# A fused attention and FFN kernel: distances spread by TensorE, single bias loads, four copies on VectorE, rounds 0 and 1 in other orders

## Chip, cores and metric

One core of a Trainium2 chip. The metric is device time in microseconds, the median of several runs; lower is better. In the text PE is TensorE, DVE is VectorE, ACT is ScalarE, POOL is GpSimd and SP is SyncE, which here only issues DMAs.

## What is computed

Attention with a bias made by a small MLP from the logarithm of the distance, then a softplus feed-forward network over the result. Shapes: 4 batches, 8 heads, 576 positions, head size 64; the MLP has 32 hidden units; the network goes 512 to 2048 to 512.

```python
x = log1p(|i - j|) / log1p(max(i, 1))          # 576 x 576
bias = relu(x[..., None] @ w1 + b1) @ w2        # one 576 x 576 map for each of 8 heads
attn = softmax(q @ k.T / 8 + bias)
o = attn @ v                                    # to 2304 x 512
h = o @ w_in
out = (max(h, 0) + log1p(exp(-|h|))) @ w_out
```

## The kernel before

The program is one long straight line of instructions. The author writes the order of each engine by hand, so every engine works strictly in the order of the text, and an instruction that waits holds up all that stands behind it on its engine. SP's DMA issues are such a queue too.

**Start.** Three small DMAs bring the MLP's weights (`wts`, line 188), the row of 576 log distances copied to all 128 partitions (`dist`, line 189) and a table (`tab`, line 190). DVE makes `lw` (distances times w1, line 198), `pb1` (line 199) and `coef` (line 200) of them. All later work of the bias hangs on `lw`.

**Bias stage.** 36 steps, `s` from 0 to 35, make 16 rows of all 8 bias maps each. DVE or ACT makes four relu tiles `m` for a step (lines 220 and 222), PE multiplies them with `coef` into an accumulator `acc` in PSUM (line 235; two of these), ACT copies it in two pieces into a tile `e` (line 256; five of these), and SP stores `e` to a scratch `e_d` in HBM (line 260). The bias is read back from `e_d` in tiles of 128 rows: tiles 0 to 3 are the first head of a pair, 5 to 8 the second, tile 4 the last 64 rows of both (lines 305, 307, 309, 310). Each tile needs eight steps of the store to have landed. Tiles 0 and 5, 1 and 6, 2 and 7 are loaded in pairs after steps 10, 18 and 26. Tiles 3, 8 and 4 stand behind the loop in the text.

Into the late steps the first scores of attention are woven (`STAGE`). A number `wt` there means round `w`, tile `t`. `D` computes scores on PE (line 346), adds the bias and finds the row maximum on DVE (line 364) and takes the exponential on ACT (line 382). `R` computes the scores and only copies them out of PSUM, on ACT (line 357), to be finished later.

**Rounds.** Attention runs in rounds 0 to 16; round `n` is one batch of one pair of heads. A round is written as a string of tokens, each a few instructions. `S`, `A`, `X` and a digit are scores (PE), bias and maximum (DVE) and exponential (ACT) of one tile of the next round; `Z`, `ZA`, `ZX` the same for the round itself. `T` with two digits is a set of transposes on PE, `V` the copy of the result to SBUF, on ACT (`/a`, line 315) or DVE (`/d`, line 317). `P` is a product with v (line 469); `P3` and `P4` belong to the round before. `I` inverts the row sums on DVE (lines 507, 508), and needs the round's nine exponentials. `R` transposes them on PE, `C` copies them on ACT (line 523) and stores them to `r_d` in HBM (line 524). A third step reads them back, spread over 64 partitions each, by three DMAs into a tile `rb` (line 530): in rounds 0 and 1 on ACT's queue, later on SP's. `O` multiplies the accumulated product of the round before with its `rb` on DVE (line 489), which frees the accumulator `o` in PSUM for PE. Four DMAs then store the result to `x_d` (lines 495 to 498). `L` is a small copy on POOL, `B` one step of preparing FFN weights, `D6` and `D14` are 6 and 14 transposes of the identity with no use of their result, `k`, `q`, `v`, `w`, `b` are loads, `G` is the `rb` load, `Y` the store of the result, `W` a store of prepared weights.

Rounds 2 to 13 all use the same string `ROUND`; rounds 0 and 1 have their own, with their loads placed by position (`LOADS0`, `LOADS`). Where a round is not in `STEADY`, the reading back of `rb` is put off by 24 tokens from `C`, the store of the result by 8 tokens from `O`, and the store of prepared weights by 8 tokens from `B4`:

```python
STEADY = range(2, 17)
...
            if tok == "C" and n not in STEADY:
                defer(RB_AFTER, lambda n=n: units["r", n][2]())   # RB_AFTER = 24
```

**FFN.** From about 270 us on, PE multiplies without a break (lines 784 and 842).

Of the kernel before, what the change touches and what calls it, by code (L numbers as in the profile page):

```python
# [51 lines left out]
SETS = ((2, 4), (3, 8), (7, 5, 6), (1, 0))  # L52

ROUND0 = """
A6 A2 Z7 T10/1 A7 Z3 T20/0 V20/a T30/o A0 T00/2 ZA7 V00/d V30/a V10/a A1 A5 D6 Z8 X7 X2 ZX7 ZA3 X5
X6 ZA8 A3 ZX3 ZX8 Z4 ZA4 ZL1 ZL3 ZX4 A8 D14 T22/2 T40/1 T32/o ZL4 V32/d T02/0 V22/a V02/a T01/o X0
T11/2 V40/d T21/1 V11/a ZL2 V01/d V21/d L2 T12/0 P0 X8 L0 X1 I V12/d T41/1 A4 P1 X4 T31/0 R/2
V41/a C P2 V31/d L3 X3 L4 L1
"""

ROUND1 = """
I S4 T20/0 S3 A4 T11/1 A3 T00/2 S2 P3 X4 V00/d V20/a T02/0 V11/d T12/2 V02/a R/1 C P4 T41/0 S7
T22/1 S0 A2 O V12/a T01/o V41/a T10/0 V22/d L4 B0 T21/2 V01/a X3 A7 S1 V10/d P0 V21/a A0 T31/0
X2 T32/2 S5 X7 A1 P1 S6 V31/a V32/d X0 S8 B1 T30/1 X1 B2 L0 A5 T40/0 V30/a B3 L1 A8 V40/a X8 A6
X6 L3 P2 B4 X5 L2
"""

ROUND14 = """
# [56 lines left out]
def tile_log_bias_attention__then__softplus_ffn(  # L125
# [139 lines left out]
    N = 16  # L265
# [53 lines left out]
    def u_s(n, t):  # L319
# [187 lines left out]
        nc.vector.tensor_scalar(s_, s_, 1e-9, None, op0=ALU.add)  # L507
        nc.vector.reciprocal(s_, s_)

    def queue(n):  # L510
        return nc.scalar if n < 2 else nc.sync

    def u_r(n):

        st_ = {}

        def pe(on=None):
            assert ("i", n) in done
# [17 lines left out]
        return pe, first, second  # L536
# [33 lines left out]

    units = {}

    def raw_(w, t):
        unit = units["s", w, t] = u_s(w, t)
        return [((1,), unit[0], unit[3])]

    def emit(n, tok):

# [26 lines left out]
        elif kind in ("R", "C"):  # L605
            stage(("r", n), u_r, "RC".index(kind), *on)
        elif kind == "O":
            if n:
                stage(("x", n - 1), u_x, 0)
                if n not in STEADY:  # L610
                    defer(8, lambda: stage(("x", n - 1), u_x, 1))
        elif kind == "B":
            i = min(n, N - 1) - 1
            if 0 <= i < len(pre):
                stage(("b", i), u_bits, *a)
                if a[0] == 4 and n not in STEADY:
                    defer(8, lambda: stage(("b", n - 1), u_bits, 5))
        elif kind in ("k", "q"):
            emit_load(n + 3, kind)
        elif kind == "v":  # L620
            emit_load_v(n + 2)
        elif kind == "w":
            pre_load(n)
        elif kind == "b":
            if tiles:
                emit_bias(*tiles.pop(0))
        elif kind == "G":
            units["r", n][2]()
# [338 lines left out]
    for n in range(N + 1):  # L967
        tiles = [(n // B + 1 + (n % B == 3), t) for t in SETS[n % B]]
        if n < 3:
            tiles = [(1, t) for t in ((), range(5), range(5, 9))[n]]  # L970
        if n == 1:
            assert not s_held
            s_use[0] = 0
        toks = {0: ROUND0, 1: ROUND1, N - 2: ROUND14, N - 1: ROUND15, N: ROUND16}.get(n, ROUND).split()
        for i, tok in enumerate(toks):
            load = {0: LOADS0, 1: LOADS}.get(n, LOADS if n > N - 2 else {}).get(i)
            if load in ("k", "q"):
                emit_load(n + 3, load)
            elif load == "v":
                emit_load_v(n + 2)  # L980
            elif load == "v1":
                emit_load_v(n + 1)
            elif load == "w":
                pre_load(n)
            elif load == "b" and tiles:
                emit_bias(*tiles.pop(0))
# [88 lines left out]
```

## Time and profile before

| | us |
|---|---|
| median of 3 runs | 678.45 (677.08 to 681.55) |
| the profiled execution | 677.26 |
| its span, first to last instruction | 675.5 |
| granted TensorE clock over the span | 0.991 of 2.4 GHz |
| PE, ACT, DVE busy | 642.0, 512.2, 499.2 |

The span falls into four parts: the start (to 7 us), the bias stage (to 62 us), 17 rounds (to some 270 us) and the FFN. All times below are from the profiled execution, counted from its first instruction. Busy times of PE are modelled, so a PE that is shown busy need not be at its peak.

### The profile page before, as it was taken

The numbers are of one execution on the slowest core, as the hardware profiler recorded it, in microseconds if no ns is written. First come the engines' busy times: TensorE is split into PE (matmuls) and PEld (weight loads), VectorE is DVE, ScalarE is ACT, GpSimd is POOL, SyncE is SP. The second block draws the span as 40 slices with busy tenths as digits, with TensorE's granted clock in tenths as the row PEclk, the third lists the DMA queues.
The fourth block names the chain that finished last, engine by engine and source line by source line (L and its number), as shares of the span: only waits on it lengthen the run. The fifth ranks groups of instructions, "written<-read, shape, count | busy, mean of one in ns | idle before, by whom it ended". The sixth has DMA issues, their size and how long they took to land.

```text
span 675.5 us, 13207 instructions
## 1 busy us (share of the span) xinstructions
PE 642.0 (95%) x4807; PEld 478.2 (71%) x4807; DVE 499.2 (74%) x1082; ACT 512.2 (76%) x1058; POOL 38.0 (6%) x106
## 2 busy tenths in 40 slices
PE   5689779999999998899999999999999999999997
PEld 2124447667667665588888888888888888888886
DVE  6986668999999997779785965796774555556564
ACT  6898769999999997677776867786775665665654
POOL 0000111111111111100000000000000000000000
PEclk9989799999999999999999999999999999999999
DMA  4876948879788545451410305030300502204020
GB/s 146 298 266 221 360 137 277 264 251 297 248 266 278 179 149 187 154 187 64 155 64 32 125 1 188 31 125 14 112 1 0 187 1 93 95 0 156 0 95 32
DMA packets 51041, 96.85 MB, mean 143 GB/s; under 512 B 7440, under 2 KB 19104, under 8 KB 50976
## 3 DMA queue, kind: packets, MB, share of 16 engines
q1 hardware_dynamic: 50208, 95.34, 41.9%
q8 instruction: 38, 0.62, 0.4%
q10 hardware_dynamic: 768, 0.66, 0.3%
q14 instruction: 27, 0.22, 0.1%
HBM read 67.98 MB, written 28.01 MB: 142 GB/s over the span
## 4 chain that ended last, share of the span: by engine, by line
PE 89%; ACT 5%; DMA 3%; DVE 2%; issue 1%; ACTq 1%; SPq 0%; DVEq 0%
PE y L842 29%; PE h L784 29%; PE o L469 10%; PE s L346 6%; PE s L410 4%; PE acc L235 4%; PE t L346 3%; ACT p L382 2%; PE t L410 1%; ACT e L256 1%; DMA e_d<-e 1%; PE o L346 1%; PE o L410 1%; DMA dist<-in_c_dist_dram 1%; ACTq L530 0%
## 5 line engine op out<-in xcount | busy, mean ns | idle before, releaser
L784 PE MATMUL h<-x,wi 128*128 128x512 f32 (+1 forms) x960 | 212.5, 370 | 2.0 <-DVE wi L757 1.4
L842 PE MATMUL y<-wo,g 128*128 128x512 f32 x864 | 209.7, 391 | 0.0
L784 PEld LDWEIGHTS h<-x,wi 128*128 128x128 f32 x960 | 169.1, 189 | 36.4 <-DVE wi L757 2.6
L842 PEld LDWEIGHTS y<-wo,g 128*128 128x128 f32 x864 | 161.2, 188 | 33.7 <-DVE g L816 0.2
L807 DVE SCALAR_TENSOR_TENSOR u<-u,e 128x512 f32<-128x512 f32 (+1 forms) x80 | 50.9, 637 | 104.9 <-ACT l L804 104.7
L382 ACT ACTIVATE p<-p,m 128x576 f32<-128x576 f32 x144 | 110.4, 768 | 5.3 <-DVE m L364 1.8
L800 ACT ACTIVATE e<-h 128x512 f32<-128x512 f32 (+1 forms) x80 | 44.2, 553 | 80.4 <-PE h L784 80.4
L469 PE MATMUL o<-pt,vn 128*64 128x256 f32 (+3 forms) x640 | 82.9, 419 | 1.2 <-DVE pt L317 1.2
L364 DVE CUSTOM_DVE_ANT_0 p<-s,b 128x576 f32<-128x576 f32 x79 | 58.4, 753 | 9.7 <-ACT e L256 3.3
L814 ACT ACTIVATE g<-l 128x512 fp32r<-128x512 f32 (+1 forms) x80 | 46.8, 585 | 20.3 <-DVE l L811 10.7
L346 PE MATMUL s<-kn,qn 64*128 64x288 f32 (+1 forms) x416 | 58.5, 415 | 0.2 <-ACT p L357 0.2
L469 PEld LDWEIGHTS o<-pt,vn 128*64 128x64 f32 (+1 forms) x640 | 37.4, 136 | 29.0 <-issue 8.0
L816 DVE TENSOR_TENSOR g<-l,g 128x512 fp32r<-128x512 f32 (+1 forms) x80 | 50.3, 628 | 3.7 <-ACT g L814 3.7
L235 PE MATMUL acc<-m,coef 128*32 128x512 f32 (+17 forms) x352 | 36.9, 521 | 16.1 <-ACT e L256 8.6
L315 ACT ACTIVATE pt<-s 128x384 f32<-128x384 f32 (+1 forms) x93 | 44.2, 483 | 8.4 <-ACT r L523 4.5
L811 DVE TENSOR_TENSOR l<-l,u 128x512 f32<-128x512 f32 (+1 forms) x80 | 50.4, 630 | 0.0
L809 DVE SCALAR_TENSOR_TENSOR l<-h,l 128x512 f32<-128x512 f32 (+1 forms) x80 | 50.4, 630 | 0.0
L804 ACT ACTIVATE l<-u 128x512 f32<-128x512 f32 (+1 forms) x80 | 47.1, 589 | 2.9
L801 ACT ACTIVATE e<-e 128x512 f32<-128x512 f32 (+1 forms) x80 | 47.2, 590 | 2.5
L803 ACT ACTIVATE u<-e 128x512 f32<-128x512 f32 (+1 forms) x80 | 47.2, 590 | 2.6
L410 PEld LDWEIGHTS s<-ident,p 64*128 64x128 f32 x672 | 32.5, 140 | 18.4 <-DVE m L364 6.7
L222 DVE TENSOR_SCALAR m<-lw,pb 128x576 f32<-128x576 f32 (+17 forms) x122 | 44.4, 446 | 0.4 <-PE acc L235 0.4
(66 smaller groups left out, 682.0 us busy)
## 6 DMA issues: line engine op xcount, KB each, us to landing
e_d<-e SPq DMA_DIRECT2D x36, 295.5 KB, 3.3
qn<-in_q_dram SPq DMA_DIRECT2D x16, 576.0 KB, 6.4
b<-e_d SPq DMA_DIRECT2D x32, 288.0 KB, 3.7
r<-in_moe_w_in_dram SPq DMA_DIRECT2D x16, 512.0 KB, 3.4
r<-in_moe_w_out_dram SPq DMA_DIRECT2D x16, 512.0 KB, 4.7
xr<-x_d SPq DMA_DIRECT2D x28, 256.0 KB, 4.5
vn<-in_v_dram SPq DMA_DIRECT2D x16, 320.0 KB
kn<-in_k_dram SPq DMA_DIRECT2D x16, 288.0 KB, 6.6
```

What stands on the lines that cost most here:

```text
L235: nc.tensor.matmul(acc[32 * g:32 * g + 32, lo:hi], lhsT=coef.rearrange("p o h -> p (o h)"), rhs=hid[s, g][:, lo:hi], start=True, stop=True ...
L346: nc.tensor.matmul(ps[at:at + w, half, :SH], lhsT=q_n[n][rows, hd, c0:c0 + w], rhs=k_n[n][rows, hd], start=True, stop=True, tile_position= ...
L364: nc.vector.tensor_tensor_reduce(prob[n, t].rearrange("p (a c) -> p a c", a=2), st_["ps"], bias[pr, t].rearrange("p (a c) -> p a c", a=2), ...
L382: nc.scalar.activation(p, p, AF.Exp, bias=st_["m"], scale=-1.0, accum_out=ssum[n][:, PLACE.index(t):PLACE.index(t) + 1],)
L410: nc.tensor.transpose(ps[:, a, i], src[rows], ident[rows, 64 * a:64 * a + 64], tile_position=(64 * a, 0))
L469: nc.tensor.matmul(o[up, half, 0:w], lhsT=v_n[n][rows, jb, hd], rhs=pt[n, jb][rows, c0:c0 + w], start=(jb == 0), stop=(jb == 4), tile_posi ...
L784: nc.tensor.matmul(ps[:, :nb], lhsT=wi[f][:, a, 128 * c:128 * c + 128], rhs=xs[bi, c][:, x_, :nb], start=(i == 0), stop=(i == 11),)
L807: nc.vector.scalar_tensor_tensor(u, u, -1.0, e, op0=ALU.add, op1=ALU.subtract)
L809: nc.vector.scalar_tensor_tensor(l, ps, 0.0, l, op0=ALU.max, op1=ALU.add)
L811: nc.vector.tensor_tensor(l, l, u, op=ALU.subtract)
L816: nc.vector.tensor_tensor(g[:, 1], l, g[:, 0], op=ALU.subtract)
L842: nc.tensor.matmul(y, lhsT=g[:, a, 128 * ts:128 * ts + 128], rhs=wo[f][:, w_], start=(first and i == 0), stop=(last and i == 2),)
```

## The change

Five edits.

1. The distances come as one row into partition 0. PE spreads them: a column of ones, one partition deep, times the row, in two products of 512 and 64 columns into a PSUM tile `wide` (one of the two `acc` buffers). `lw` reads that PSUM tile. The order of the three loads is table, weights, distances.
2. Bias tiles are loaded singly after steps 10, 13, 18, 21, 26, 29, 34 and 35 (`EARLY`); only tile 4 stands behind the loop. There the k load of round 2 comes ahead of tile 4, its q load behind v of round 0.
3. Four of the nine raw copies of round 1's scores (`V11`, `V13`, `V18`, `V14`) are on DVE, not on ACT.
4. Round 0 has another order, with its loads as tokens. `G` stands right behind `C`.
5. Round 1 uses `ROUND`, and the tiles of the next pair are loaded one in round 0, four in round 1, four in round 2. All `rb` loads are issued by SP. `STEADY` and the lines that defer work stay as they are.

```diff
 ROUND0 = """
-A6 A2 Z7 T10/1 A7 Z3 T20/0 V20/a T30/o A0 T00/2 ZA7 V00/d V30/a V10/a A1 A5 D6 Z8 X7 X2 ZX7 ZA3 X5
-X6 ZA8 A3 ZX3 ZX8 Z4 ZA4 ZL1 ZL3 ZX4 A8 D14 T22/2 T40/1 T32/o ZL4 V32/d T02/0 V22/a V02/a T01/o X0
-T11/2 V40/d T21/1 V11/a ZL2 V01/d V21/d L2 T12/0 P0 X8 L0 X1 I V12/d T41/1 A4 P1 X4 T31/0 R/2
-V41/a C P2 V31/d L3 X3 L4 L1
-"""
-
-ROUND1 = """
-I S4 T20/0 S3 A4 T11/1 A3 T00/2 S2 P3 X4 V00/d V20/a T02/0 V11/d T12/2 V02/a R/1 C P4 T41/0 S7
...
+v1 Z7 Z3 T10/o ZA7 Z8 V10/a T20/0 ZX7 ZA3 V20/a ZA8 D6 ZX3 T00/1 k q V00/d Z4 A2 ZX8 T30/2 V30/a
+T12/o V12/d A0 ZL1 ZL2 ZL3 T22/1 V22/a X2 T32/2 V32/d D14 ZA4 T02/o V02/a w T40/1 V40/d ZX4 ZL4 A1
+T01/2 X0 V01/a L0 T11/o V11/d X1 T21/1 V21/a I A7 P0 R/1 C G v A5 X7 P1 T31/2 V31/d A6 X5 T41/1
+V41/a P2 b A3 X6 X3 L1 A8 X8 A4 X4 L2 L3 L4
 """
...
-LOADS = {22: "b", 4: "q", 0: "v", 34: "w", 6: "k", 25: "b", 23: "b", 10: "b", 31: "b"}
-LOADS0 = {17: "k", 28: "v1", 71: "w", 6: "q", 59: "v"}
...
-LATE = 3
+EARLY = ((10, 0), (13, 5), (18, 1), (21, 6), (26, 2), (29, 7), (34, 3), (35, 8))
 STAGE = """
-21:D00 21:R15 24:R16 25:R10 26:R12 26:D01 27:D05 29:R17 31:R11 31:R13 32:D02 33:D06 33:R18
-34:R14
+21:D00 21:A15 24:A16 25:A10 26:A12 26:D01 27:D05 29:A17 31:V11 31:V13 32:D02 33:D06 33:V18
+34:V14
 """
...
-    nc.sync.dma_start(out=dist, in_=c_dist.to_broadcast([128, S]))
-    nc.sync.dma_start(out=tab[:, 0:212], in_=c_tab)
+    nc.sync.dma_start(out=dist[0:1], in_=c_dist)
     nc.vector.memset(one, 1.0)
+    ones = bc.tile([128, 128], F32, name="ones")
+    nc.vector.memset(ones[0:1], 1.0)
+    wide = pb.tile([128, 1024], F32, tag="acc", name="wide")
+    for lo, hi in ((0, 512), (512, S)):
+        nc.tensor.matmul(
+            wide[:, lo:hi], lhsT=ones[0:1], rhs=dist[0:1, lo:hi], start=True, stop=True
+        )
...
-    nc.vector.tensor_scalar(lw, dist, w1c, None, op0=ALU.mult)
+    nc.vector.tensor_scalar(lw, wide[:, 0:S], w1c, None, op0=ALU.mult)
...
-        def raw():
+        def raw(on="a"):
             p = prob[n, t].rearrange("p (a c) -> p a c", a=2)
-            nc.scalar.activation(p, st_["ps"], AF.Copy)
+            copy_on(on, p, st_["ps"])
...
-                queue(n).dma_start(
+                nc.sync.dma_start(
...
-    for t in (3, 8, 4):
-        emit_bias(0, t)
+    emit_load(2, "k")
+    emit_bias(0, 4)
     emit_load_v(0)
-    emit_load(2)
+    emit_load(2, "q")
...
-            tiles = [(1, t) for t in ((), range(5), range(5, 9))[n]]
+            tiles = [(1, t) for t in ((0,), (1, 2, 4, 3), (8, 7, 5, 6))[n]]
...
-        toks = {0: ROUND0, 1: ROUND1, N - 2: ROUND14, N - 1: ROUND15, N: ROUND16}.get(n, ROUND).split()
+        toks = {0: ROUND0, N - 2: ROUND14, N - 1: ROUND15, N: ROUND16}.get(n, ROUND).split()
```

## Rows read from the trace of the kernel before

**Rows 1.** Chain that ended last, rounds 2 and 3: start, length, what.

```profile
98.92 0.19 ACT p L382
99.98 1.82 PE o L469 x16
...
112.33 1.82 PE o L469 x16
```

**Rows 2.** Windows: length, busy by engine, granted clock, DMA share, GB/s.

```profile
48.00:61.02 13.02, 13.02 (x132) 5.17 (x136) 9.72 (x26) 11.51 (x26) 0.00 (x0) 1.00 0.67 218
62.00:80.20 18.20, 13.10 (x143) 7.77 (x139) 11.03 (x31) 15.39 (x40) 2.97 (x9) 0.81 0.83 310
79.60:99.70 20.10, 16.54 (x196) 9.71 (x195) 12.07 (x33) 12.93 (x33) 2.77 (x7) 1.00 0.56 182
106.81:119.16 12.35, 12.35 (x167) 8.58 (x168) 11.34 (x31) 11.67 (x30) 2.04 (x6) 1.00 0.87 283
```

**Rows 3.** Timeline of round 1, ACT with its queue, and DVE.

```profile
83.64 2.58 ACTq L530 DMA_DIRECT2D rb<-r_d  x3
86.32 0.27 ACT L523 ACTIVATE r<-s 9x128 f32<-9x128 f32 x1 [2.25 <-DMA rb<-r_d]
...
88.32 0.82 DVE L489 TENSOR_TENSOR x<-o,rb 128x256 f32<-128x256 f32 x2 [3.79 <-DMA rb<-r_d]
```

**Rows 4.** Chain that ended last, start of the program.

```profile
1.17 4.57 DMA dist<-in_c_dist_dram
...
5.85 0.52 DVE lw L198
```

**Rows 5.** Page, part 2: granted clock in 40 slices of 16.9 us.

```profile
PEclk9989799999999999999999999999999999999999
```

**Rows 6.** Timeline at the end of the bias stage: ACT, SP, DVE.

```profile
61.27 0.73 ACT L256 ACTIVATE e<-acc,tab 128x575 f32<-128x575 f32 x1
...
59.97 0.43 SPq L307 DMA_DIRECT2D b<-e_d  x1
60.44 1.90 SPq L260 DMA_DIRECT2D e_d<-e  x2
65.64 0.53 SPq L309 DMA_DIRECT2D b<-e_d  x1
...
70.21 0.76 DVE L364 CUSTOM_DVE_ANT_0 p<-s,b 128x576 f32<-128x576 f32 x1 [0.55 <-DMA b<-e_d]
```

**Rows 7.** Chain, round 0: seven exponentials with their accumulator reads.

```profile
65.77 5.29 ACT p L382 x14
```

**Rows 8.** Page, part 5: copies on ACT, bias additions on DVE, products of the bias stage.

```profile
L364 DVE CUSTOM_DVE_ANT_0 p<-s,b 128x576 f32<-128x576 f32 x79 | 58.4, 753 | 9.7 <-ACT e L256 3.3
...
L235 PE MATMUL acc<-m,coef 128*32 128x512 f32 (+17 forms) x352 | 36.9, 521 | 16.1 <-ACT e L256 8.6
L315 ACT ACTIVATE pt<-s 128x384 f32<-128x384 f32 (+1 forms) x93 | 44.2, 483 | 8.4 <-ACT r L523 4.5
```

**Rows 9.** Timeline of round 0: ACT and its queue.

```profile
78.58 0.27 ACT L523 ACTIVATE r<-t 9x128 f32<-9x128 f32 x1 [1.02 <-PE t L410]
78.88 0.54 ACTq L524 DMA_DIRECT2D r_d<-r  x1
```

**Rows 10.** Timeline of steady rounds: SP, PE, DVE.

```profile
118.56 2.16 SPq L530 DMA_DIRECT2D rb<-r_d  x3
...
124.61 1.89 PE L469 MATMUL o<-pt,vn 128*64 128x256 f32 x16
...
127.63 0.34 PE L410 MATMUL o<-ident,p 64*128 64x64 f32 x6
...
126.55 0.82 DVE L489 TENSOR_TENSOR x<-o,rb 128x256 f32<-128x256 f32 x2 [0.39 <-PE o L469]
```

**Rows 11.** Time from issue to landing of all DMAs on rb's tensors.

```profile
DMA to landing us min/median/max: 2.5/3.3/5.0
```

**Rows 12.** Chain near the last round.

```profile
260.65 3.00 DMA r_d<-r
```

More of the change, by code (lines that the diff above doesn't have):

```diff
@@ L54 @@
 ROUND0 = """
-A6 A2 Z7 T10/1 A7 Z3 T20/0 V20/a T30/o A0 T00/2 ZA7 V00/d V30/a V10/a A1 A5 D6 Z8 X7 X2 ZX7 ZA3 X5
-X6 ZA8 A3 ZX3 ZX8 Z4 ZA4 ZL1 ZL3 ZX4 A8 D14 T22/2 T40/1 T32/o ZL4 V32/d T02/0 V22/a V02/a T01/o X0
-T11/2 V40/d T21/1 V11/a ZL2 V01/d V21/d L2 T12/0 P0 X8 L0 X1 I V12/d T41/1 A4 P1 X4 T31/0 R/2
-V41/a C P2 V31/d L3 X3 L4 L1
-"""
-ROUND1 = """
-I S4 T20/0 S3 A4 T11/1 A3 T00/2 S2 P3 X4 V00/d V20/a T02/0 V11/d T12/2 V02/a R/1 C P4 T41/0 S7
-T22/1 S0 A2 O V12/a T01/o V41/a T10/0 V22/d L4 B0 T21/2 V01/a X3 A7 S1 V10/d P0 V21/a A0 T31/0
-X2 T32/2 S5 X7 A1 P1 S6 V31/a V32/d X0 S8 B1 T30/1 X1 B2 L0 A5 T40/0 V30/a B3 L1 A8 V40/a X8 A6
-X6 L3 P2 B4 X5 L2
+v1 Z7 Z3 T10/o ZA7 Z8 V10/a T20/0 ZX7 ZA3 V20/a ZA8 D6 ZX3 T00/1 k q V00/d Z4 A2 ZX8 T30/2 V30/a
+T12/o V12/d A0 ZL1 ZL2 ZL3 T22/1 V22/a X2 T32/2 V32/d D14 ZA4 T02/o V02/a w T40/1 V40/d ZX4 ZL4 A1
+T01/2 X0 V01/a L0 T11/o V11/d X1 T21/1 V21/a I A7 P0 R/1 C G v A5 X7 P1 T31/2 V31/d A6 X5 T41/1
+V41/a P2 b A3 X6 X3 L1 A8 X8 A4 X4 L2 L3 L4
 """
@@ L187, in tile_log_bias_attention__then__softplus_ffn @@
     wts = bc.tile([128, 2 + H], F32, name="wts")
+    nc.sync.dma_start(out=tab[:, 0:212], in_=c_tab)
     nc.sync.dma_start(out=wts, in_=mlp)
-    nc.sync.dma_start(out=dist, in_=c_dist.to_broadcast([128, S]))
-    nc.sync.dma_start(out=tab[:, 0:212], in_=c_tab)
+    nc.sync.dma_start(out=dist[0:1], in_=c_dist)
     nc.vector.memset(one, 1.0)
+    ones = bc.tile([128, 128], F32, name="ones")
[5 more added lines that the diff above has]
+        )
     psi, rho, blk = tab[:, 0:144], tab[:, 144:180], tab[:, 180:212]
@@ L508, in inv @@
         nc.vector.reciprocal(s_, s_)
-    def queue(n):
-        return nc.scalar if n < 2 else nc.sync
     def u_r(n):
@@ L571, in tile_log_bias_attention__then__softplus_ffn, with raw_ @@
     units = {}
-    def raw_(w, t):
+    def raw_(w, t, on="a"):
         unit = units["s", w, t] = u_s(w, t)
-        return [((1,), unit[0], unit[3])]
+        return [((1,), unit[0], lambda: unit[3](on))]
     def emit(n, tok):
@@ L618, in emit @@
         elif kind in ("k", "q"):
-            emit_load(n + 3, kind)
+            emit_load(n + (a[0] if a else 3), kind)
         elif kind == "v":
-            emit_load_v(n + 2)
+            emit_load_v(n + (a[0] if a else 2))
         elif kind == "w":
@@ L872, in tile_log_bias_attention__then__softplus_ffn @@
     emit_mm(0)
-    early = {8 * t + 7: (t, t + 5) for t in range(3)}
+    early = {s: (t,) for s, t in EARLY}
     for s in range(36):
@@ L880, in tile_log_bias_attention__then__softplus_ffn @@
             emit_load(1 + LOAD_AT.index(s))
-        for t in early.pop(s - LATE, ()):
+        for t in early.pop(s, ()):
             emit_bias(0, t)
@@ L884, in tile_log_bias_attention__then__softplus_ffn @@
         for kind, w, t in mine:
-            run((s_ if kind == "D" else raw_)(int(w), int(t)))
+            run(s_(int(w), int(t)) if kind == "D" else raw_(int(w), int(t), on=kind.lower()))
         if not mine:
@@ L973, in tile_log_bias_attention__then__softplus_ffn @@
             s_use[0] = 0
-        toks = {0: ROUND0, 1: ROUND1, N - 2: ROUND14, N - 1: ROUND15, N: ROUND16}.get(n, ROUND).split()
[L975 to L986, printed above, removed]
+        toks = {0: ROUND0, N - 2: ROUND14, N - 1: ROUND15, N: ROUND16}.get(n, ROUND).split()
+        for tok in toks:
             emit(n, tok)
```

## Prediction

> **What bounds the kernel now.** I read the chain that ended last first, to find from where on the time is fixed. P3 of round 2 starts at 99.98 and P3 of round 3 at 112.33, 12.35 us later [rows 1]. The window of one such round shows PE busy for all of its 12.35 us [rows 2]: from round 2 on PE sets the pace, and the change touches nothing there. So it can only move one mark, the start of P3 in round 2, and every us there is a us of the total.
>
> Then I read the windows ahead of the mark. Round 1 fills 79.6 to 99.7, 20.1 us, with PE busy for 16.54 and ACT for 12.93 [rows 2]: this stage is not bound by an engine, it waits. The timeline shows for what. ACT's queue issues the three `rb` loads for 2.58 us from 83.64, and ACT stands still for 2.25 us until it is through; DVE waits 3.79 us and multiplies round 0's result at 88.32, when `rb` has landed [rows 3]. Round 0, 62.0 to 80.2, holds 15.39 us of ACT, 13.10 of PE, 11.03 of DVE [rows 2]: ACT is nearest to the bound. The last 13.02 us of the bias stage have PE busy throughout, ACT for 11.51, DVE for 9.72 [rows 2]. At the start all waits for `dist`: issued at 1.17, landed 4.57 us later; `lw` runs from 5.85 for 0.52 and ends at 6.37 [rows 4].
>
> **The start.** The copy of `dist` to 128 partitions goes; one row of 2.3 KB, third in SP's queue where the table was (issue at about 1.6, behind two issues of 0.43), comes. The trace has no such small load. Its landing lies between 2.5 us, the quickest of the loads on `rb`'s tensors [rows 11], and the 4.57 us of `dist`: 4.1 to 6.2; I take 4.3, near the small end, since it is the smallest load. PE then spreads it: 512 columns and 64, each product in two instructions, 0.5 to 1.0 us (one instruction of this stage has a mean of 0.52, [rows 8]); I take 1.0, since one waits for the end of the last. `lw` from PSUM costs between 0.52 (from SBUF, [rows 4]) and the 0.75 of a bias addition, which reads PSUM [rows 8]; I take 0.75. So `lw` ends at 4.3 + 1.0 + 0.75 = 6.05, 0.3 earlier than 6.37; with the ends 5.1 to 8.0, a gain of 1.2 to a loss of 1.6. The table, now first, is no later than it was.
>
> A rule of the skill speaks against this part. The trace grants TensorE nine tenths or more of its clock in the first 16.9 us [rows 5], so the first products there were not at the lower level for long. The Trainium skill, TensorE: Matmul & The Clock Gate, section "What's actually happening", says that half speed is the default until there has been activity; by that the spreading would take twice as long, and the start would lose 0.7 us in place of gaining 0.3. The row speaks against it.
>
> **The end of the bias stage.** Single loads and DVE's copies: nothing, since PE is busy without a gap from 48 to 61 [rows 2], and its work stays. A raw copy of 576 columns on ACT lies between the 0.48 us of 384 columns [rows 8] and the 0.756 of an exponential (5.29 / 7, [rows 7]); four are 1.9 to 3.0 us, which would be gained if PE's cover were gone. On DVE they cost 0.75 each, as the bias additions do; DVE has 13.02 - 9.72 = 3.3 us free. So ACT ends the last `e` at 62.0 as before [rows 6], less the 0.3.
>
> **Round 0.** Bias tiles 3 and 8 now stand behind steps 34 and 35 in SP's queue; in the trace one of them (59.97) is issued ahead of the last two stores, though the text has it behind them [rows 6]. Tile 8 thus goes at about 62.4 and, at tile 4's price (65.64 to 70.21, 4.57 us, [rows 6]), lands at 67. ACT has 3.9 us of work ahead of its exponential (four exponentials, two copies, prices below), so it idles from 65.9 to 67.7, then has 2.9 us more (`ZX8`, `V30`, `V22`, `X2`, `V02`), to 70.6. Tile 4 has to wait for the last store as before and lands at 70.2 again, and its bias addition (0.75, [rows 8]) ends at 70.95: later than 70.6, so tile 8 costs nothing. The k load put ahead of it, and the other loads behind it, fill that wait and cost nothing; if SP's k load were late, tile 4 would be late by its 0.45.
>
> In the new order ACT does tile 4's exponential before most of round 1's, and the rest of the round hangs on it: from 70.95, nine exponentials (`ZX4`, `X0`, `X1`, `X7`, `X5`, `X6`, `X3`, `X8`, `X4`) at 0.756 = 6.8, three copies at 0.45 = 1.35, and `C` with its DMA issue, 0.9 [rows 9]. The end is 80.0. Without any wait ACT would be through with its 15 exponentials, 8 copies and `C` at 62.0 + 11.3 + 3.2 + 0.7 = 77.2, a bound 2.7 earlier. With as much idling as the 2.8 us of before (18.20 - 15.39, [rows 2]) it is also 80.0. I take that, and 81.3 as the other bound: tile 4's landing may vary as the landings on `rb`'s tensors do, by half of 5.0 - 2.5 [rows 11].
>
> **Round 1.** In round 2 the last exponential ends at 99.11 and P3 starts at 99.98, 0.87 us later [rows 1]. Round 1 with the same order then has P3 at 80.0 + 0.87 = 80.9. If it ran as a steady round, P3 of round 2 would come 12.35 later, at 93.2: a gain of 6.8.
>
> **What is done twice.** `STEADY` still begins at 2, so rounds 0 and 1 keep their deferred steps beside the new tokens. In round 0 `rb` is loaded behind `C` by `G`, and 24 tokens later, with `L4`, again, into the other buffer; `O` of round 1 reads the second. In round 1 `rb`, the store of the result and the store of the weights are also doubled (three, four and one DMAs), some 5 us more on SP beside a round; those have a whole round until someone needs them, and I cost them at nothing.
>
> The first pair is not covered. `C` on ACT comes after `V21` (`I`, `P0` and `R` ahead of it need `ZX4` and fit beside ACT's work until then): 70.95 + 3 x 0.756 + 2 x 0.45 = 74.1; the store of `r_d` is issued 0.3 later [rows 9] and lands 3.0 after that [rows 12]: 77.4. SP stands still for it, with v, b and the second `rb` set queued behind. Three `rb` issues take 2.16 [rows 10], v and b 0.45 each [rows 6], so the second set starts at 80.5, its third DMA at 82.1; landing 2.5 to 5.0, median 3.3 [rows 11]: 85.4. In a steady round `O` starts 1.94 us after P3 (126.55 against 124.61), and PE's next transposes into `o` follow 0.26 us after its end [rows 10]; so there is next to no slack. `O` is due at 82.8 and can run at 85.4: PE loses 2.6 us, which it can't make up at full occupancy. Behind `O` on DVE stand the next bias additions, so ACT runs dry too. Ends: none, if the landing is quick and the round late; 7.4, if both landings take 5.0, both sets 2.58 and the store 0.24 more (0.54 for 0.3). ACT's waits of 2.25 and DVE's of 3.79 [rows 3] are gone, but this one takes their place.
>
> **The sum.** Mark before 99.98. After: 80.0 + 0.87 + 12.35 + 2.6 - 0.3 = 95.5. Gain 4.5. Profiled execution 677.26 - 4.5 = 672.8; it lies 1.2 below the median of the runs, so the median is 678.45 - 4.5 = 674.0.
>
> **Rivals.** (a) The second `rb` load is hidden, because the transfers are done in 2.5 us and round 0 ends later than ACT's sum, or because ACT idles less: no stall, 671.3; with a round 0 at its bound of 77.2, 668.5. For it: before, DMA was busy 0.83 in round 0 [rows 2], and fewer loads stand ahead of `rb` now. Against it: five issues between landing and the last copy are SP's own time.
>
> (b) The clock. In round 0 the granted clock was 0.81 [rows 2], which is (1 - 0.81) x 18.2 / 0.5 = 6.9 us at 1.2 GHz; slice 5 of the page shows the dip, slice 6, in which DVE waits its 3.79 us [rows 3] and round 1's PE idles for most of 20.1 - 16.54 = 3.6 us [rows 2], shows none [rows 5]. If the 2.6 us stall in round 1 brings it on, 6 us at half speed in a round in which PE is full cost 3 us more: 677.0. The same page and section of the Trainium skill say that an idle array is gated down again; by that this rival would be the rule, and slice 6 is against it.
>
> (c) Slower than before: the `rb` chain. SP has to get through `r_d`'s landing and two sets. Without the stall the mark is 6.8 + 0.3 = 7.1 earlier; so from the point at which `O` starts 7.1 us late, at 89.9, the change loses. At the stall's upper end of 7.4 (landings of 5.0 behind a DMA system still full of loads) it is slower by 0.3, 678.8; with the start's loss of 1.6 for its gain of 0.3, 680.7.
>
> (d) The change doesn't do what it says: round 1 isn't steady since the loads for its scores, now behind SP's wait, are late. They are issued by 70 in both, and were in time for 79.6 before; I count it with (c).
>
> **How the numbers follow.** Forecast 0.45 (674.0, own range 672 to 676); (a) 0.27; (b) 0.18; (c) and (d) 0.10. The range 669.5 to 678 takes in the forecast, (a) with most of its better end, (b), and the ends of the start; (c) stays out. One per cent is 6.8 us, about what a measurement of this kernel tells from no change: faster by more is 671.7 or less, which is most of (a), 0.22; slower by more than 685.2 only if (c) meets a bad start, 0.03; the rest, 0.75, lies within.
>
> **What would show it.** `lw` ends near 6.05. ACT ends the last `e` near 61.7. DVE adds tile 4's bias near 70. Round 0's last exponential ends near 79.7. Six `rb` issues on SP from 77, none on ACT; DVE's first multiplication waits for DMA and starts near 85; PE has a hole of 2 to 3 us ahead of it. P3 of round 2 near 95.5, then 12.35 a round. I am wrong if the hole is not there (the second load is ahead of `O`), if round 0's end moves by more than 1.5 us, or if P3 to P3 from round 2 on differs from 12.35.

## The result, and the profile after

| | before | after | predicted |
|---|---|---|---|
| median of the runs, us | 678.19 (675.83 to 684.29, 15 runs) | 682.68 (680.26 to 686.6, 15 runs) | 674.0 (669.5 to 678.0) |
| profiled execution, us | 677.26 | 683.61 | 672.8 |
| its span, us | 675.5 | 681.5 | |
| P3 of rounds 2, 3 and 4 by the timeline, us | 99.91, 112.26, 124.61 | 94.95, 110.77, 130.03 | 95.5, 107.85, 120.2 |

After stands to before as 1.0055, with a 95% interval of 1.0034 to 1.0077: slower by half a per cent, where a gain of 4.5 us was forecast. The mark on which the forecast was built, P3 of round 2, came out within 0.6 us, by luck, as two errors ahead of it cancel (shown below); the rounds behind it did not. The timeline of TensorE in the kernel after, its products with the values (P3 and P4 are the rows of 16):

```profile
82.60 1.89 PE L467 MATMUL o<-pt,vn 128*64 128x256 f32 x16
...
94.95 1.89 PE L467 MATMUL o<-pt,vn 128*64 128x256 f32 x16
...
110.77 1.89 PE L467 MATMUL o<-pt,vn 128*64 128x256 f32 x16
...
130.03 1.89 PE L467 MATMUL o<-pt,vn 128*64 128x256 f32 x16
```

Round 1 takes 12.35 us from P3 to P3, as predicted. In the kernel before it took 17.9, from the row below to 99.91:

```profile
82.02 1.19 PE L469 MATMUL o<-pt,vn 128*64 128x256 f32 x8
```

So P3 of round 2 is 5.0 us earlier than before. Then come 15.82 and 19.26 us where before and prediction have 12.35: rounds 2 and 3 lose 3.47 + 6.91 = 10.4 us. So 5.0 are gained and 10.4 lost, 5.4 of the 6.0 us by which the two spans differ. What ended the waits between 82 and 125 us of the kernel after (total, times, longest):

```profile
ACT pt L313 <- DMA rb<-r_d: 9.0, 2, 5.0
PEld s L344 <- ACT pt L313: 8.2, 2, 4.6
DVE x L487 <- DMA rb<-r_d: 8.0, 2, 4.5
PE s L344 <- ACT pt L313: 7.1, 2, 4.0
```

They are one event in two rounds: `rb` lands late, ACT and DVE both stand for it at the same time, and PE stands for ACT. Why `rb` is late can be read in the queue of SP:

```profile
85.00 0.33 SPq L493 DMA_DIRECT2D x_d<-x  x1
...
88.98 0.47 SPq L495 DMA_DIRECT2D x_d<-x  x1
...
90.45 0.33 SPq L493 DMA_DIRECT2D x_d<-x  x1
...
93.23 1.87 SPq L525 DMA_DIRECT2D rb<-r_d  x3
...
95.77 1.73 SPq L525 DMA_DIRECT2D rb<-r_d  x3
...
99.98 4.86 SPq L705 DMA_DIRECT2D w_d<-a  x2
104.93 0.38 SPq L692 DMA_DIRECT2D r<-in_moe_w_in_dram  x1
...
110.67 3.65 SPq L525 DMA_DIRECT2D rb<-r_d  x3
```

And the chain that ended last, in the same stretch:

```profile
85.00 5.44 DMA x_d<-x
...
99.98 4.47 DMA w_d<-a
...
105.86 7.03 DMA qn<-in_q_dram
...
112.91 2.86 DMA rb<-r_d
```

SP's own waits, from 80 to 126 us:

```profile
SPq L705 <- DMA w_d<-a: 4.1, 1, 4.1
SPq L495 <- DMA r_d<-r: 3.1, 1, 3.1
SPq L525 <- DMA qn<-in_q_dram: 2.6, 2, 1.7
...
SPq L493 <- DMA x_d<-x: 0.3, 1, 0.3
```

All that round 1 does twice is seen here: the result (85.00 and 90.45), `rb` (93.23 and 95.77), the weights (two issues within 4.86). A second store goes to the place of the first, and the chain shows that it is issued only when the first has landed, 5.44 and 4.47 us after that one's issue. For the weights SP stood still for 4.1 of these. In the 5.44 of the result it stood for 3.1 at the third DMA of the first set, until ACT's `r_d` had landed, and only the last 0.3 for the result itself (with the weights stored once 0.6 and 3.3). Behind it in the queue wait `rb` of round 1, the loads, and `rb` of round 2, issued only from 110.67 on. The second of those three loads stood 1.7 us more, until the load of q that was issued at 105.86 had landed, though it doesn't read it. On ACT and DVE:

```profile
99.32 0.49 ACT L313 ACTIVATE pt<-s 128x384 f32<-128x384 f32 x1 [3.99 <-DMA rb<-r_d]
...
110.88 0.27 ACT L518 ACTIVATE r<-t 9x128 f32<-9x128 f32 x1
115.85 0.27 ACTq L519 DMA_DIRECT2D r_d<-r  x1
116.16 0.49 ACT L313 ACTIVATE pt<-s 128x384 f32<-128x384 f32 x1 [5.02 <-DMA rb<-r_d]
```

```profile
84.54 0.82 DVE L487 TENSOR_TENSOR x<-o,rb 128x256 f32<-128x256 f32 x2 [0.27 <-PE o L467]
...
100.02 0.82 DVE L487 TENSOR_TENSOR x<-o,rb 128x256 f32<-128x256 f32 x2 [3.52 <-DMA rb<-r_d]
...
116.84 0.82 DVE L487 TENSOR_TENSOR x<-o,rb 128x256 f32<-128x256 f32 x2 [4.46 <-DMA rb<-r_d]
```

Two things are to be read. In round 1 the multiplication at 84.54 waits for PE and not for a DMA: the hole of 2.6 us that the prediction put there is absent, and the DVE wait of [rows 3] is gone. And ACT's store of round 3's `r_d` stands from 111.15 to 115.85 until `rb` of round 2 is down, although it doesn't use what this load brings. So `rb` has two deadlines: the next store of `r_d`, about when P3 starts, and the `O` 1.94 us behind P3. The windows show what comes on top (columns as in [rows 2]):

```profile
67.90:78.00 10.10, 8.49 (x63) 4.64 (x65) 5.56 (x17) 6.65 (x17) 0.59 (x2) 0.50 0.67 231
...
112.70:116.00 3.30, 0.00 (x0) 0.00 (x0) 0.00 (x0) 0.00 (x0) 0.00 (x0) 0.93 0.62 184
116.00:123.00 7.00, 6.29 (x62) 4.38 (x64) 3.16 (x8) 5.02 (x13) 0.50 (x2) 0.54 1.00 338
```

In round 3 no engine works for 3.3 us, and then the granted clock is 0.54 for 7 us: 6.29 us of PE at 0.54 instead of 1.00 are 6.29 x 0.46 = 2.9 us. With the 4.0 us for which PE stood that is the 6.9 of round 3. In round 0 the clock is at 0.50, the 1.2 GHz level, for 10 us.

The start and the end of the bias stage, the rows that answer to [rows 4] and [rows 6]:

```profile
1.65 0.33 SPq L181 DMA_DIRECT2D dist<-in_c_dist_dram  x1
...
3.10 2.36 PE L187 MATMUL wide<-dist,ones 1*128 1x512 f32 x4 [3.10 <-DMA dist<-in_c_dist_dram]
...
5.49 0.82 DVE L196 TENSOR_SCALAR lw<-wide,wts 128x576 f32<-128x576 f32 x1 [4.47 <-PE wide L187]
...
59.94 0.90 ACT L254 ACTIVATE e<-acc,tab 128x16 f32<-128x16 f32 x2 [1.35 <-PE acc L233]
...
74.61 0.27 ACT L518 ACTIVATE r<-s 9x128 f32<-9x128 f32 x1 [1.84 <-PE s L408]
...
80.87 0.76 ACT L380 ACTIVATE p<-p,m 128x576 f32<-128x576 f32 x1
```

`lw` ends at 6.31 (6.37 before), the last `e` at 60.84 (62.0), round 0's last exponential at 81.7.

### The profile page after: what moved, and what is told of

Read it like the earlier page. It is cut to its first block, busy times and chain, and to the rows that moved or that the text cites. A ratio compares the mean times of both kernels' runs of the same rounds, so it can differ in the third digit from the quotient of the medians.

```text
span 681.5 us, 13238 instructions
## 1 busy us (share of the span) xinstructions
PE 648.4 (95%) x4811; PEld 482.8 (71%) x4811; DVE 502.0 (74%) x1086; ACT 510.6 (75%) x1055; POOL 37.4 (5%) x106
## 4 chain that ended last, share of the span: by engine, by line
PE 85%; DMA 6%; ACT 3%; DVE 2%; SPq 2%; issue 1%; ACTq 0%; DVEq 0%
PE y L837 29%; PE h L779 28%; PE o L467 9%; PE s L344 5%; PE s L408 3%; PE acc L233 3%; PE t L344 3%; DMA e_d<-e 2%; PE t L408 1%; DMA qn<-in_q_dram 1%; PE o L344 1%; ACT e L254 1%; DMA x_d<-x 1%; PE o L408 1%; ACT p L380 1%
## 5 line engine op out<-in xcount | busy, mean ns | idle before, releaser
L809 ACT ACTIVATE g<-l 128x512 fp32r<-128x512 f32 (+1 forms) x80 | 46.8, 585 | 20.4 <-DVE l L806 10.7
L344 PEld LDWEIGHTS s<-kn,qn 64*128 64x128 f32 (+1 forms) x412 | 31.7, 173 | 20.5 <-ACT pt L313 8.2
```

Of the source, the lines that this page charges most:

```text
L344: nc.tensor.matmul(ps[at:at + w, half, :SH], lhsT=q_n[n][rows, hd, c0:c0 + w], rhs=k_n[n][rows, hd], start=True, stop=True, tile_position= ...
```

## The experiments

Theory A, from these rows: SP works its queue in order; what is doubled in round 1 makes it late; lateness up to a slack is hidden, what exceeds it is lost, and a long standstill brings the half clock too. Rivals: the second `rb` set of round 0 (the prediction's hole); a fixed price for each doubled store; the new order of round 0, the start or the loads. In the diffs "-" is the kernel after, unless another is named; "..." stands for lines left out.

**Nothing twice.**

```
-STEADY = range(2, 17)
+STEADY = range(0, 17)
```

> Nothing is done twice (STEADY from 0). Theory A: the steps doubled in round 1 put SP's queue so far behind that rb of rounds 1 and 2 land late, and this costs the 3.5 us by which P3 of round 3 and the 7.0 us by which P3 of round 4 came late; without them P3 stays at 95 in round 2 and then comes every 12.35, and the time is 682.7 - 10.4 = 672.3. Rival B: the steady order in round 1 is too much for SP by itself (four bias tiles, four loads, rb on SP): rounds 2 and 3 keep more than half of their loss, 677 or more.

672.0 us (670.85 to 672.19) beside 679.01 before; ratio 0.988 [0.9864, 0.9897]. The timeline of PE shows the rounds 12.35 us apart from round 2 on; under it SP's queue:

```profile
94.64 1.89 PE L467 MATMUL o<-pt,vn 128*64 128x256 f32 x16
...
106.98 1.89 PE L467 MATMUL o<-pt,vn 128*64 128x256 f32 x16
...
119.33 1.89 PE L467 MATMUL o<-pt,vn 128*64 128x256 f32 x16
...
93.81 0.33 SPq L705 DMA_DIRECT2D w_d<-a  x1
94.23 0.38 SPq L692 DMA_DIRECT2D r<-in_moe_w_in_dram  x1
...
99.98 2.76 SPq L525 DMA_DIRECT2D rb<-r_d  x3
```

By the medians the doubled steps cost some 10.7 us, and the rest of the change gains 7. SP reaches the weight load at 94.23 (104.93 in the kernel after) and `rb` of round 2 at 99.98 (110.67): 10.7 us of lateness in the queue, with P3 of round 2 within 0.3 of the same time.

**Only round 0's `rb` twice.**

```
-STEADY = range(2, 17)
+STEADY = range(1, 17)
```

> Only rb of round 0 is loaded twice (STEADY from 1). Theory A: as with nothing twice, within 0.7: 672.3 to 673, since that load was there in time for O. Rival C: the second load of round 0 starts SP's lateness: 676 or more.

672.16 us (671.76 to 673.97), ratio 0.9892 [0.9876, 0.9909]; P3 at 82.00, 94.35, 106.69, and `O` of round 1 at 83.93 without a wait for a DMA. The pair on which the prediction spent 2.6 us costs nothing that can be measured by itself; the loss comes with round 1's. It does make SP later: the store of the result stood 2.5 us for the landing of `r_d` here, a wait that is absent with nothing twice, and the issues of round 1's `rb` ended 3.0 us ahead of P3 of round 2 in place of 6.0.

**Two of the three doubled in round 1.** Weights stored once, result stored once, `rb` loaded once:

```
 weights once
-                if a[0] == 4 and n not in STEADY:
+                if a[0] == 4 and n not in STEADY and n != 1:
 result once
-                if n not in STEADY:
+                if n not in STEADY and n != 1:
 rb once
-            if tok == "C" and n not in STEADY:
+            if tok == "C" and n not in STEADY and n != 1:
```

Weights once: 

> All doubled but the store of prepared weights in round 1. Theory A: SP is free 4.9 us earlier after it; round 2 keeps its 3.5 us, as its rb stands ahead of that store, round 3 loses 2 in place of 7: 677.7. Rival B: no change, 682.7.

Result once: 

> All doubled but the store of round 0's result in round 1. Theory A: rb of round 1 goes 3.1 us earlier, so round 2's loss falls from 3.5 to about 0.5, and round 3's by about as much: 676.5. Rival B: no change, 682.7.

`rb` once: 

> The changed kernel, with only the loads of rb in round 1 done once; both stores of round 1 stay doubled. Theory A (lateness adds up on SP, and only what exceeds a slack of some 3.5 us is lost): result store alone cost 1.2, weight store alone 1.0; together rb of round 2 comes some 4 us later than with the result store alone (103.3), at 107, for an O due at 110: holes of 1.2 and 2 to 3 us, and the half clock behind the second, 675 to 677.5. If the costs of the two stores simply add: 674.2. If the second rb costs nothing in company either: 682, as the changed kernel.

**One of the three alone**, on top of nothing twice:

```
 only the weights
+                if a[0] == 4 and n == 1:
 only the result
+                if n == 1:
 only rb
+            if tok == "C" and n == 1:
```

Weights: 

> Nothing is doubled but the weight store of round 1. Theory A (SP's queue has a slack, and only what exceeds it is lost): the second weight store waits some 4.5 us for the first one's landing, rb of round 2 then issues at 103.5 in place of 99.98 and lands at 108.3 to 109, about when the O of round 3 (108.9) wants it; a hole of 0 to 1 us, 672.0 to 673.5, P3 of rounds 2 and 3 at 94.6 and 107.0, of round 4 within 1 us of 119.3. Theory B (a doubled store costs its whole wait): 676.5, P3 of round 4 at 123.8.

Result: 

> Nothing is doubled but the result store of round 1. Theory A (slack): the second set waits for the first one's landing to about 88.9, rb of round 1 issues at 91.6 in place of 86.93 and lands by 96, before the O of round 2 at 96.6 wants it; SP has caught up by its next idle time. 672 to 673, P3 of round 3 at 107.0 to 107.8. Theory B (a doubled store costs its whole wait): 677, P3 of round 3 at 112.

`rb`: 

> Nothing is doubled but the loads of rb in round 1. With slack theory A: the second set takes SP 1.8 us, and SP stands idle for some 3 us ahead of the weight store, so nothing: 672.0, P3 of rounds 2, 3 and 4 at equal distances of 12.35. If the second set (which waits for no store) holds lanes that ACT's r_d store needs: a hole of 1 to 2 us in round 2, 673 to 674.

What rounds 2 and 3 lose is the distance of P3 of round 4 from P3 of round 2, less 2 x 12.35:

| doubled in round 1 | P3 of round 2, of round 4 | lost in rounds 2 and 3 | median, us | ratio to before |
|---|---|---|---|---|
| nothing | 94.64, 119.33 | 0.0 | 672.0 | 0.988 [0.9864, 0.9897] |
| `rb` | 96.21, 120.90 | 0.0 | 672.52 | 0.9913 [0.9882, 0.9945] |
| weights | 93.77, 119.43 | 1.0 | 673.49 | 0.9928 [0.9906, 0.995] |
| result | 93.60, 119.60 | 1.3 | 673.39 | 0.9936 [0.9919, 0.9953] |
| `rb` and weights | 94.15, 124.88 | 6.0 | 678.35 | 0.9991 [0.9971, 1.001] |
| `rb` and result | 93.46, 125.47 | 7.3 | 677.89 | 0.9976 [0.9965, 0.9988] |
| result and weights | 96.61, 125.71 | 4.4 | 679.15 | 1.001 [0.9992, 1.0028] |
| all three | 94.95, 130.03 | 10.4 | 682.68 | 1.0055 [1.0034, 1.0077] |

Alone they lose 0, 1.0 and 1.3, 2.3 in sum; all together 10.4. A price for each store doesn't give that. The last four rows also load round 0's `rb` twice, which alone loses nothing.

A slack does give it, and the timelines show its size. For these eight kernels and the one with only round 0's `rb` twice, take the rounds 1, 2 and 3: when the last issue of the round's `rb` ended, and when the next round's P3 started. In 18 of the 27 cases the issues ended 1.44 us or more ahead of P3, and P3 of the round behind came 12.35 later, without loss. In the other nine they ended later, and each lost:

| end of the issues of `rb` less start of P3 (negative: ahead of it), us | -1.09 | -1.07 | -0.60 | -0.42 | 2.05 | 2.31 | 2.55 | 3.55 | 4.06 |
|---|---|---|---|---|---|---|---|---|---|
| lost in that round, us | 0.7 | 0.15 | 1.0 | 1.15 | 4.4 | 5.3 | 3.5 | 6.9 | 7.3 |

So theory A holds. The loss is the lateness beyond -1.44 within some 0.6 us, and 0.9 to 1.9 us more in the four rounds whose granted clock was below 1.00 (0.82 to 0.90; the rows with 4.4, 5.3, 6.9 and 7.3).

The split between the rounds was wrong for weights once: 3.5 and 2 us expected, 7.3 and 0 measured, all in round 2, so that its total of 677.89, close to the 677.7 expected, is luck. Result once came out 1.9 us above the 676.5 expected. Of the 7.3, the half clock is part (windows of that kernel):

```profile
95.40:98.00 2.60, 0.00 (x0) 0.00 (x0) 0.00 (x0) 0.00 (x0) 0.00 (x0) 1.00 0.75 221
98.00:105.00 7.00, 4.62 (x40) 3.09 (x42) 3.15 (x8) 3.62 (x9) 0.29 (x1) 0.51 0.90 278
```

`rb` once lost 4.4 us in rounds 2 and 3, within 1 us of the 3.2 to 4.2 expected, but its total is 1.6 above the range. The difference is in round 1, 16.29 us from P3 (80.32) to P3 (96.61):

```profile
84.73 0.82 DVE L487 TENSOR_TENSOR x<-o,rb 128x256 f32<-128x256 f32 x2 [2.73 <-DMA rb<-r_d]
```

That is the hole of the prediction, in size and in place, in a kernel that has round 0 in common with the one after. Of the 3.9 us that this round took above 12.35, PE stood for 2.1 and was busy 1.8 longer, at a granted clock of 0.90 over the round. In the kernel after `O` starts at 84.54, 0.2 earlier, but P3 comes at 82.60 in place of 80.32.

**The order of round 0.** The old order with its loads where they stood, and the steady round 1 (the old string as in front, with the tokens `q k v1 v w b` for its loads):

```
-STEADY = range(2, 17)
+STEADY = range(1, 17)
...
-V41/a P2 b A3 X6 X3 L1 A8 X8 A4 X4 L2 L3 L4
+T01/o X0 T11/2 V40/d T21/1 V11/a ZL2 V01/d V21/d L2 T12/0 P0 X8 L0 X1 v I V12/d T41/1 A4 P1 X4 T31/0
+R/2 V41/a C P2 V31/d w L3 X3 L4 L1 b
```

> Round 0 in its old order, with its loads where they stood, round 1 in the steady one with nothing twice in it, the rest of the change kept. If the new round 0 matters only through the early turn of the sums: r_d stored at about 78.9 in place of 73, rb issued at 80.2 to 82 and landed by 85, for an O due at 84.0: a hole of 0.5 to 1.5 us, 672.6 to 673.5, P3 of round 1 at 82 and of round 2 at 95 to 96. If rb goes as late as on ACT before (83.64): a hole of 2.5 to 3 us, 674.6 to 675. If the new order does nothing: 672.0.

671.65 us (670.35 to 672.98), ratio 0.9904 [0.988, 0.9928]: as with the new order, and nearest to the last of the three cases in its total, though not in its mechanism. The new order is worth nothing measurable here. P3 of round 1 came at 79.04, 3 us earlier than expected and than before with the same order (82.02), for which no run here isolates the cause. Round 1 then took 14.76 us, as the hole at `O` was larger than expected:

```profile
83.54 0.82 DVE L487 TENSOR_TENSOR x<-o,rb 128x256 f32<-128x256 f32 x2 [2.88 <-DMA rb<-r_d]
```

**The other parts.** The distances by DMA, all copies on ACT, the bias tiles in pairs, each with nothing twice (with the distances by DMA, the ones, `wide` and its products go, and the three loads stand in their old order):

```
 distances by DMA
-    nc.sync.dma_start(out=dist[0:1], in_=c_dist)
+    nc.sync.dma_start(out=dist, in_=c_dist.to_broadcast([128, S]))
...
-    nc.vector.tensor_scalar(lw, wide[:, 0:S], w1c, None, op0=ALU.mult)
+    nc.vector.tensor_scalar(lw, dist, w1c, None, op0=ALU.mult)
 copies on ACT
-21:D00 21:A15 24:A16 25:A10 26:A12 26:D01 27:D05 29:A17 31:V11 31:V13 32:D02 33:D06 33:V18
-34:V14
+21:D00 21:A15 24:A16 25:A10 26:A12 26:D01 27:D05 29:A17 31:A11 31:A13 32:D02 33:D06 33:A18
+34:A14
 pairs
-    early = {s: (t,) for s, t in EARLY}
+    early = {8 * t + 7: (t, t + 5) for t in range(3)}
...
-        for t in early.pop(s, ()):
+        for t in early.pop(s - 3, ()):
...
-    emit_bias(0, 4)
+    for t in (3, 8, 4):
+        emit_bias(0, t)
```

Distances: 

> Nothing twice, and the distances spread by a DMA to all 128 partitions as before, not by TensorE. The product lw ended at 6.31 with TensorE's spreading and at 6.37 with the DMA, so by the traces: no change, 671.8 to 672.6 beside 672.0 with nothing twice. If the start were worth what the prediction put down for it (0.3): 672.3, which the measurement can hardly tell. A loss of 1 us or more would say that the spreading does something besides the start (TensorE's clock, the loads of tab and weights one place earlier).

Copies: 

> Nothing twice, and all nine raw copies on ACT. In the changed kernel the last e ends 1.1 us earlier than before (60.84 against 62.0). If the four copies on VectorE are what brought that: the last e at 61.5 to 62, and 0 to 1 us in the total (672.0 to 673.0), 0 if round 0 hides it behind its half clock. If it came from the loads instead: the last e stays at 60.8, and 672.0.

Pairs: 

> Nothing twice, and the bias tiles of head pair 0 loaded in pairs as before, 3, 8 and 4 after the stage. If the loads are hidden, as the prediction says: 672.0. If the early landing of tiles 3 and 8 is what lets round 0 end earlier (with the old round 0 and single loads P3 of round 1 is at 79.0, against 82.0 in the kernel before): biases 3, 8 and 4 land 2 to 4 us later, round 0 ends 1 to 3 us later, 673 to 675.

671.55, 671.21 and 672.37 us; 0.9889 [0.9868, 0.9911], 0.9889 [0.9869, 0.991] and 0.9904 [0.9883, 0.9925], beside 0.988 with nothing undone. None is worth anything measurable. So edits 1 to 4, undone one at a time, don't carry the 7 us; edit 5 is left, and the rows of round 1 show what it gains, 17.9 to 12.35. No run undoes the four together. The last `e` ends at 61.18 with the distances by DMA and with all copies on ACT, and at 61.62 with the pairs. In the kernel after and the twelve other runs whose bias stage is the same it ends between 59.15 and 60.84, so 0.3 to 0.8 beyond that scatter is all that can be seen; the totals don't follow it.

**The turn of the sums earlier.** In the new order, R, C and the `rb` loads ahead of P0, T31 and T41 ahead of P1, nothing twice:

```
-T01/2 X0 V01/a L0 T11/o V11/d X1 T21/1 V21/a I A7 P0 R/1 C G v A5 X7 P1 T31/2 V31/d A6 X5 T41/1
-V41/a P2 b A3 X6 X3 L1 A8 X8 A4 X4 L2 L3 L4
+T01/2 X0 V01/a L0 T11/o V11/d X1 T21/1 V21/a I R/1 C G T31/2 V31/d A7 T41/1 V41/a A5 X7 v P0 A6 X5 P1 P2 b A3
+X6 X3 L1 A8 X8 A4 X4 L2 L3 L4
```

> Nothing twice, and in round 0 the turn of the sums ahead of P0, T31 and T41 ahead of P1, which run at half clock at 2.2 us each. If the waits of ACT (1.84) and DVE (3.65) behind P0 and P1 set the end of round 0: the last exponential ends 1 to 2 us earlier, P3 of round 1 at 80.5 to 81.5, total 670 to 671. If PE's own work at half clock sets it: P3 of round 1 at 82.3 as with nothing twice, total 672.0. If P0 to P2 come late instead and push P3: 673.

670.59 us (669.12 to 670.96), ratio 0.9884 [0.9862, 0.9906], P3 of round 1 at 79.43 and of round 2 at 91.78, 2.9 earlier than with nothing twice. The expectation's 82.3 was counted back from round 2; by the timeline P3 of round 1 with nothing twice is at 80.68, 1.25 later than here. The other 1.6 are a stretch at the lower clock that the profiled execution with nothing twice had in round 1 (82 to 84, granted clock 0.51), and by the ratios the two can't be told apart.

In the old order the same ("-" is here the kernel with the old order; `STEADY` begins at 0, since `G` stands in the string):

```
-X8 L0 X1 v I V12/d T41/1 A4 P1 X4 T31/0 R/2 V41/a C P2 V31/d w L3 X3 L4 L1 b
+X8 L0 X1 v I R/2 C G V12/d T41/1 A4 P1 X4 T31/0 V41/a P2 V31/d w L3 X3 L4 L1 b
```

> The old order of round 0 with its turn of the sums moved up behind the sums (ahead of V12, T41, P1) and rb issued behind it at once, nothing twice. With the old order rb landed at 83.5 for an O due at 81.0, and DVE waited 2.88 for it. If that wait is the whole cost: r_d stored at about 74, rb landed by 79, P3 of round 1 at 79.0 and of round 2 at 91.4, total 669.2 (668.5 to 670). If the earlier turn stalls ACT and DVE behind the sums as long as it saves: 671.5.

A miss: 675.52 us (673.93 to 677.29), ratio 0.9956 [0.9938, 0.9973]. `rb` was in time, but the weight load `w` had come to stand behind it in SP's queue:

```profile
77.02 1.73 SPq L525 DMA_DIRECT2D rb<-r_d  x3
78.79 0.58 SPq L692 DMA_DIRECT2D r<-in_moe_w_in_dram  x1
...
83.99 0.66 ACT L667 ACTIVATE a<-r 128x512 f32<-128x512 f32 x1 [4.21 <-DMA r<-in_moe_w_in_dram]
```

```profile
82.50:86.00 3.50, 0.31 (x4) 0.30 (x8) 1.17 (x4) 1.66 (x4) 0.61 (x1) 0.89 1.04 410
86.00:92.00 6.00, 6.00 (x58) 4.08 (x52) 2.67 (x7) 4.02 (x11) 0.51 (x2) 0.50 0.71 221
```

With `w` and `b` moved ahead of the turn ("-" is the kernel just shown):

```
-X8 L0 X1 v I R/2 C G V12/d T41/1 A4 P1 X4 T31/0 V41/a P2 V31/d w L3 X3 L4 L1 b
+X8 L0 X1 v w b I R/2 C G V12/d T41/1 A4 P1 X4 T31/0 V41/a P2 V31/d L3 X3 L4 L1
```

> As the old order with the early turn, with the weight load and the bias load moved ahead of rb in SP's queue (there ACT waited 4.21 us for the weight load that stood behind rb, and the clock fell). If that place in the queue was the whole loss: no wait of ACT for r in round 1, rb landed by 81 for an O due at 82, P3 of round 2 12.35 behind that of round 1, at 91.5 to 92.7, total 669.5 to 671.2. If the early turn itself costs: 673 or more.

669.87 us (669.76 to 670.38) beside 679.15, ratio 0.9877 [0.9852, 0.9902], the best median of the study, though by the ratios not to be told from nothing twice (0.988). The place of the two loads in the queue was the whole loss of the miss; neither wait is left:

```profile
68.14 0.73 SPq L692 DMA_DIRECT2D r<-in_moe_w_in_dram  x1
...
76.57 1.73 SPq L525 DMA_DIRECT2D rb<-r_d  x3
...
81.83 0.82 DVE L487 TENSOR_TENSOR x<-o,rb 128x256 f32<-128x256 f32 x2 [0.32 <-PE o L467]
```

## Why the prediction was wrong

**The step that failed** is the one under "What is done twice" on round 1: "some 5 us more on SP beside a round; those have a whole round until someone needs them, and I cost them at nothing". The 5 us of issues were right (the second sets take 2.7, 1.73 and 0.33). What was missed is that a second store is issued only when the first has landed, 5.44 and 4.47 us after its issue, and that SP stands still in much of this (4.1 us for the weights; for the result 0.3, behind 3.1 for `r_d`). So SP reached the weight load 10.7 us later than with nothing twice, not 5 later. And it isn't the doubled steps' data that are needed soon, but what stands behind them in the queue: `rb` of round 1 and of round 2. The pattern was in the prediction, for round 0, where SP stands still for `r_d` "with v, b and the second `rb` set queued behind". It wasn't carried to round 1. The step cost 10.4 us where 0 stood. With it falls the premise at the head of the prediction, that the change can move only the start of P3 in round 2: from 1.4 us ahead of the next P3 on, a late `rb` moves every round behind it.

**The hole of 2.6 us at `O`** is right in its mechanism, but whether it opens depends on when P3 comes. The second set was issued by 80.79 (82.1 forecast) in the kernel after, and `O` started at 84.54 (85.4 forecast); P3 came at 82.60, 2.0 later than forecast (80.9 less 0.3), and there was nothing left to wait for. Where P3 came at 80.32, near the forecast, DVE waited 2.73, and where it came at 81.69 (result once), 0.52. A term that is the difference of two times is not a fixed 2.6 when one of them lay between 80.32 and 82.60 in the nine kernels that have this round 0.

**Round 0** ended at 81.7, not 79.7. PE was at half clock from 67.9 to 78 and its P0 and P1 took 2.19 us each; ACT's `C` waited 1.84 us behind P0, and DVE 3.65 behind P1. The prediction's sum is of ACT's durations alone: it let `P0` and `R` "fit beside ACT's work" and put the wait for PE at nothing. With the turn ahead of P0 and P1, P3 of round 1 came at 79.43, ahead of all nine, so these waits have a part in it; the totals don't tell. The late end (2.0) and the missing hole (2.6) cancelled, 94.95 against 95.5: luck. The bound of 77.2 also takes eight copies at 0.40 and `C` at 0.7; at the text's own 0.45 and 0.9 it is 77.8.

**The steady round 1** is right: 12.35 us in place of 17.9. That is 5.5 us, where the sum has 6.8 from P3 of round 2 at 99.98 to 93.2. Rival (a) without its stall, 671.3, is what nothing twice measured, 672.0. But the 7 us between the medians are only 5.3 in the traces (99.91 to 94.64 for P3 of round 2), as the profiled execution of the kernel before (677.26) lies 1.8 below the median of 679.01.

**The start** gained 0.06, not 0.3: by the chain the row was there 1.3 us after its issue (less than the lower end of 2.5), the spreading took 2.36 for 1.0, `lw` 0.82 for 0.75; the early row hid the late spreading. The 1.0 came from a mean over 18 shapes ([rows 8]): in the kernel after, a product of 512 columns takes 0.60 from 20 us on and one of 64 columns 0.22, so two of each are 1.6. For the spreading the rule of the Trainium skill, TensorE: Matmul & The Clock Gate, section "What's actually happening", which the prediction set aside for the row [rows 5], gave the better time: by it the spreading would have been twice as long as the 1.0. The two products of 512 columns took 1.12 each, 1.9 times the 0.60. The granted clock of the stretch reads 1.00 all the same, so no row here shows that the clock was the reason.

**The end of the bias stage** was 0.9 us earlier than forecast, 60.84 for 61.7, and with the same bias stage up to 2.5 earlier (59.15). Undoing the row, the copies or the loads each gave 61.2 to 61.6, not the 62.0 of before, and nothing in the total depends on it; the cause stays open.

**Rival (b)**, the clock after a stall, was held at 0.18, since slice 6 of [rows 5] shows no dip. It came, but in other rounds: after some 4 us of standstill in round 3 here, and after a stall in round 2 with the weights stored once. In round 1 it came with the weight load behind `rb`, behind the hole with `rb` once, and with nothing twice, where no hole was. The 3 us for which PE stood in round 2 of the kernel after and the hole of 2.88 with the old order (granted clock 1.00 over the round) brought none. So the dip is real, and what decides it in a given round stays open.

**Rival (c)** had the sign and the mechanism, an `rb` that SP issues too late, but for the wrong round, and with 0.10 that it shared with (d).

## What to carry to other kernels

A DMA that costs an engine nothing still costs its queue: ask of every one that is added whether it must wait for an earlier transfer, above all one to the same place, and then who needs what stands behind it. Lateness in a queue is free up to a slack and paid about in full beyond it, so edits that are each nearly free (0, 0, 1.0 and 1.3 us here) can cost 10.4 together; sum the lateness first, and compare with the slack once. When a round is taken into a steady schedule, the list that says which rounds are steady has to go with it: here one number, 10.7 us.

## Not expected of the hardware

A store to the same DRAM place as an earlier one was issued only when the earlier one had landed, 5.44 us (result) and 4.47 us (weights) after its issue, and all later DMAs of that queue were held with it.

A DMA can also be held for the landing of one whose data it doesn't use. ACT's 4.5 KB store of `r_d` stood 4.7 us (111.15 to 115.85) for `rb` loads that SP had issued; an `rb` load on SP stood 1.7 us for a q load, and a store of the result on SP 3.1 us for ACT's store of `r_d`. The profile names the landings as what ended the waits; why the program makes these DMAs wait for them no run here isolates.

A DMA of one row of 2.2 KB landed in 1.3 us, against 2.5 for the quickest of the loads in [rows 11]. And the first two products of 512 columns took 1.12 us each at a granted clock of 1.00, against 0.60 for those from 20 us on.
